# Softmax sums reciprocated through a DRAM scratch and multiplied on GpSimd, a first head put in place by engines, and a new plan

## Chip, cores and metric

The kernel runs on one NeuronCore of one Trainium2 chip. The metric is the device time of one launch in microseconds (us), 781.72 before as the median of three runs (781.61 to 781.91). Lower is better. The engines are called PE (TensorE), DVE (VectorE), ACT (ScalarE), POOL (GpSimd) and SP (SyncE, which here only issues DMAs).

## The reference

Two batches of eight attention heads, 768 positions, 64 columns, with a mask by hash bucket, and then two feed-forward blocks on the 1536 x 512 result:

```python
q_bits = (np.einsum('bhsd,dk->bhsk', q, proj) > 0)          # 6 bits, the same for k
mask = q_bucket[:, :, :, None] == k_bucket[:, :, None, :]
scores = np.where(mask, scale * np.matmul(q, k.transpose(0, 1, 3, 2)), -1e9)
attn = np.exp(scores - np.max(scores, axis=-1, keepdims=True))
attn = attn / (np.sum(attn, axis=-1, keepdims=True) + 1e-09)
x = (attn @ v).transpose(0, 2, 1, 3).reshape(1536, 512)
...
h = x @ w_in;  x = (h * np.tanh(softplus(h))) @ w_out         # block 1, 512 -> 2048 -> 512
h = x @ w_in2; y = elu(h) @ w_out2                            # block 2
```

## The kernel before, in words

**Precision.** Every fp32 operand is split into a high part rounded to fp32r and the rest, and a product is two or three matmuls over these parts. So each tensor needs a cast (line 231 on ACT, 233 on DVE and POOL) and a subtraction (`sub`, line 236).

**A head.** There are 16 heads in 8 pairs. `prepare(g)` loads k and q of head g, transposed, into `rw`, splits them into `z` (two parts), and forms `qkt`, four slots of 128 x 768 in which k and q parts are stacked for the score matmuls. Rows of `z` must change partitions for that, so four DMAs copy them (line 350, `qkt<-z`); for head 0 the four are shared between the queues of SP and ACT. The projection `pj` (line 363, six matmuls) gives the hash bits, which DVE turns into mask rows: for head 0 straight into `qkt` by four instructions (`direct`, line 370), for the others into `bits` (line 376), from which four DMAs (line 382) carry them to `qkt`.

**A tile.** `tile_ops(i)` handles 128 queries, six tiles to a head: four score matmuls into PSUM (`st`, line 418), the maximum on DVE (`pt`, line 421), its negative (`nb`, line 424), and the exponential on ACT (line 426), which also writes the row sum into a column of `sm`. After a head's last tile DVE adds 1e-9 to the six sums (line 434) and takes reciprocals (`rc`, line 437), and POOL spreads `rc` over 64 columns (`rb`, line 440). `value_ops` works on two tiles: transposes (`tu`, line 468), split by ACT and DVE into `pth` and `ptl`, and value matmuls (`xt`, line 481), which ACT copies into `xr` (line 501).

**A pair of heads.** The value result of a head lies in two halves over the partitions. DMAs carry halves to `xs` and `xr` (lines 507, 511, 513), POOL adds them (line 515). Then PE transposes `rb` into PSUM (`r`, line 493, three transposes for each half of 768 columns), DVE multiplies `r` onto `xr` (line 522), and `xr` is split into `x_hi` and `x_lo`, the operands of the first feed-forward block. The last two heads (`late`) do this in pieces of two tiles.

**Feed-forward.** Weights come in 64 units, fetched as int64 pairs and rebuilt by ACT, DVE and POOL. `h` (line 593) is 2304 matmuls of 128 x 512.

**Order.** Nothing is scheduled by hand. `Plan.run` simulates five in-order engines with the costs given to `p.op`, picks by priority (tile number plus the offsets in `OFF` and `ODD`), and writes each engine's instructions in that order. On the chip each engine runs its list strictly in order and waits on semaphores, so an instruction that waits holds up all behind it.

Of the kernel before, what the change touches and what calls it, by code (L numbers as in the profile page):

```python
# [35 lines left out]
WARM = 10  # L36
HOLD = 16
NEARLY = 3
# [3 lines left out]
WAIT = {'PE': 150, 'ACT': 0, 'DVE': 50, 'POOL': 50, 'SP': 100}  # L42
OFF = {'rh': 27.75, 'cp': -6.25, 'ld': 29.75, 'sp': 10.0, 'pj': -5.5, 'bits': -10.0, 'mk': 41.25, 'v': -55.25, 'S': -2.5, 'max': 1.25, 'exp': 15.0, 'sum': 1.25, 'T': 0.0, 'hi': -8.25, 'lo': 1.75, 'R': -10.0, 'pv': 4.0, 'xc': -12.75, 'xa': -5.75, 'xn': -33.75, 'xh': 30.25, 'xm': 29.0}
ODD = {'lo': [-2.0, -0.5, -2.5, -7.5, -7.0, 1.5], 'T': [-4.5, 1.5, 0.5, 2.0, 11.0, 0.5], 'pv': [5.5, 1.5, 2.5, -0.5, -6.0, 0.0], 'exp': [0.0, 1.5, -3.0, 1.5, 4.0, -4.5], 'hi': [3.0, 1.0, -2.5, 0.5, 6.5, 0.0], 'S': [-0.5, 1.5, 1.0, 0.0, -1.0, 0.0], 'xc': [4.0, 1.0, 7.0, 0.0, 2.5, -1.5], 'max': [1.0, 9.0, -1.0, -0.5, 1.0, 0.0]}
PE, ACT, DVE, POOL, SP = "PE", "ACT", "DVE", "POOL", "SP"
# [131 lines left out]

CH = {'rh': ('POOL',), 'v': ('POOL',), 'xh': ('ACT', 'POOL'), 'eps': ('DVE',)}

# [7 lines left out]
def kernel(ctx, tc, qk, v, w, tab, out):  # L187
    nc = tc.nc
# [97 lines left out]

    def attention(p, ap, pss, pst, psx, h_r):
        ident = ap.tile([128, 128], F32, name="ident")
# [45 lines left out]
        def prepare(g):  # L334
# [14 lines left out]
            def move(out, in_):  # L349
                return lambda e: (nc.scalar if e == ACT else nc.sync).dma_start(out=f32(out()), in_=f32(in_()))  # L350
            two = {SP: 650, ACT: 400} if g == 0 else {SP: 650}
            deps = [p.op(two, move(lambda: wt.tile[0:64, 0:2], lambda: z.tile[64:128, 0:1].to_broadcast([64, 2, S])),
                         [h], [z, wt], at('cp'), lat=4600),
                    p.op(two, move(lambda: wt.tile[64:128, 2], lambda: z.tile[0:64, 0]), [h], [z, wt], at('cp'), lat=4600),
                    p.op(two, move(lambda: wt.tile[0:64, 2:4], lambda: z.tile[0:64, 0:2]), [lo], [z, wt], at('cp'), lat=4600),
                    p.op(two, move(lambda: wt.tile[64:128, 0], lambda: z.tile[64:128, 1]), [lo], [z, wt], at('cp'), lat=4600)]
            pj = Buf(xt_r, f"pj{g}")
# [9 lines left out]
            if g == 0:  # L367
# [4 lines left out]
                for c, k in ((0, 1), (1, 1), (0, 0), (1, 0)):  # L372
                    deps.append(p.op({DVE: dve(HS)}, lambda e, c=c, k=k: direct(e, c, k), [o], [pj, wt], at('bits')))
            else:
# [13 lines left out]
            if g % 2 == 0:  # L388
# [9 lines left out]
                V[g // 2] = (vr, vt, ld, lo)  # L398

        def tile_ops(i):  # L400

# [4 lines left out]
            if t == 0:  # L406
                SM[g] = Buf(sm_r, f"sm{g}"), []
                RC[g] = Buf(rc_r, f"rc{g}")
            if g % 2 == 0 and t == 0:
                RB[g // 2] = Buf(rb_r, f"rb{g}"), {}  # L410
            sm, sums = SM[g]
            rc = RC[g]
            rb, ready = RB[g // 2]
# [16 lines left out]
            rest.append((pt, o))  # L430
            late = g >= BH - 2
            if t == NQ - 1 or late and t % 2:
                r = slice(t - 1 if late else 0, t + 1)
                s = p.op(pick('eps', {DVE: 70, POOL: 250}), lambda e: eng(e).tensor_scalar(
                    out=sm.tile[:, r], in0=sm.tile[:, r], scalar1=1e-9, scalar2=None, op0=ALU.add),
                    sums[r], [sm], order(i, 'sum'))
                s = p.op({DVE: 76}, lambda e: nc.vector.reciprocal(out=rc.tile[:, r], in_=sm.tile[:, r]),
                         [s], [sm, rc], order(i, 'sum'))
                n = r.stop - r.start
                s = p.op({POOL: 150 + 50 * n}, lambda e: nc.gpsimd.tensor_copy(  # L440
                    out=rb.tile[:, r, g % 2], in_=rc.tile[:, r].unsqueeze(2).to_broadcast([128, n, 64])),
                    [s], [rc, rb], order(i, 'sum'))
                for j in range(r.start, r.stop):
                    ready.setdefault(j, []).append(s)
            if t % 2 == 1:
# [6 lines left out]
        def value_ops(i):  # L452
# [31 lines left out]
            pv_op = x  # L484
            rb, ready = RB[g // 2]

            def spread(name, ts, after):

                r = Buf(xt_r, name)

                def run(e):
                    for j, tt in enumerate(ts):
                        nc.tensor.transpose(r.tile[:, j * 128:(j + 1) * 128],
                                            rb.tile[:, tt].rearrange("p h d -> p (h d)"), ident)
                return r, p.op({PE: 108 * len(ts)}, run, [after] + [d for tt in ts for d in ready[tt]], [rb, r], order(i, 'R'))
            b, kt = divmod(g // 2, NX)
            if g < BH - 2:
                if t == 1:
                    XR[g] = (Buf(xr_r, f"xr{g}"), [])
                xr, parts = XR[g]  # L500
                parts.append(p.op({ACT: act(TH)}, lambda e: copy(e, xr.tile[:, cs], xt.tile[:, 0:TH]), [x], [xt, xr],
                                  order(i, 'xc')))
                if t < NQ - 1:
                    return
                if g % 2 == 0:
                    xs = Buf(xs_r, f"xs{g}")
                    XS[g // 2] = xs, p.op({SP: 650}, lambda e: nc.sync.dma_start(out=xs.tile[0:64], in_=xr.tile[64:128]),
                                          parts, [xr, xs], order(i, 'xm'), lat=3000)
                    return
                xe, (xs, m) = XR[g - 1][0], XS[g // 2]  # L510
                m2 = p.op({SP: 650}, lambda e: nc.sync.dma_start(out=xs.tile[64:128], in_=xr.tile[64:128]),
                          parts, [xr, xs], order(i, 'xm'), lat=3000)
                m = p.op({SP: 650}, lambda e: nc.sync.dma_start(out=xe.tile[64:128], in_=xr.tile[0:64]),
                         parts + [m], [xr, xe], order(i, 'xm'), lat=3000)
# [3 lines left out]
                norms = []  # L518
                for c in range(2):
                    r, o = spread(f"r{i}_{c}", range(3 * c, 3 * c + 3), a)  # L520
                    hc = slice(c * HS, (c + 1) * HS)
                    norms.append(p.op({DVE: dve(HS)}, lambda e, r=r, hc=hc: nc.vector.tensor_tensor(  # L522
                        out=xe.tile[:, hc], in0=r.tile[:, 0:HS], in1=xe.tile[:, hc], op=ALU.mult), [a, o], [xe, r], order(i, 'xn')))
                h = p.op(pick('xh', {ACT: act(S, False), DVE: 500, POOL: 830}), lambda e: copy(e, x_hi[:, kt, to], xe.tile),
                         norms, [xe], order(i, 'xh'))
# [39 lines left out]

        first = []
        last, gates = [], []
        setup()
        prepare(0)
        for i in range(len(steps)):  # L570
# [136 lines left out]
    with tc.manual_schedule():  # L707
        p = Plan()
        with ExitStack() as low:
            with ExitStack() as att, ExitStack() as scores:  # L710
                def space_pool(stack, name, bufs, space=None, **kw):
                    return stack.enter_context(tc.tile_pool(name=name, bufs=bufs, **({"space": space} if space else {}), **kw))
                ap = space_pool(att, "ap", 1)
                pst = space_pool(att, "pst", TB, PSUM)
                psx = space_pool(att, "psx", 4 - TB, PSUM)
# [12 lines left out]
                h_r = Ring(6, bank)  # L728
                attention(p, ap, pss, pst, psx, h_r)
                ta = p.run()  # L730
# [54 lines left out]
```

## Time and profile before

| | |
|---|---|
| median of three runs | 781.72 us |
| the profiled execution, whole | 781.22 us |
| its span, first to last instruction | 779.4 us |
| PE busy | 761.2 us (98%) |
| DVE, ACT, POOL busy | 602.6, 416.6, 287.0 us |
| mean granted TensorE clock | 0.993 of 2.4 GHz |
| attention, to where `h` runs unbroken | 0 to 259.49 us |
| feed-forward, unbroken matmuls | 516.20 us |

The span is what the trace covers; 1.8 us of the whole time lie outside it. A profile lists when each instruction started and how long it took. "Idle before" is the time in which its engine had nothing running, with the instruction whose semaphore ended it. PE instructions are pipelined: a matmul's duration is longer than the step from its start to the next one's.

### The profile page before, as it was taken

Reading aid. Unit: us, or ns where it says so; the run is one execution under the profiler, and the core shown is the slowest. Engines: PE = TensorE matmul, PEld = TensorE weight load, DVE = VectorE, ACT = ScalarE, POOL = GpSimd, SP = SyncE. Lnnn points to the kernel's source line nnn. Section 1 sums busy time; section 2 is a strip of 40 time slices with the busy share of each in tenths; the row PEclk is TensorE's granted clock in tenths of the full one; section 3 lists DMA queues with packets and bytes.
Section 4 is the critical chain, followed back from the end, with each engine's and each line's share of the span. In section 5 each row is a group of like instructions: output and inputs, shape, how many; then the busy total and the mean of one; then the engine's idle time right before and its main releaser. Section 6 shows DMA issues by size and latency. Waiting matters only on the chain.

```text
span 779.4 us, 11177 instructions
## 1 busy us (share of the span) xinstructions
PE 761.2 (98%) x4010; PEld 660.3 (85%) x4010; DVE 602.6 (77%) x1107; ACT 416.6 (53%) x800; POOL 287.0 (37%) x228
## 2 busy tenths in 40 slices
PE   7999999999899999999999999999999999999998
PEld 6999898998897888888888888888888888888886
DVE  4899898988799865456677766899976789989852
ACT  1797787777687654453333434357555444444420
POOL 1625427516214242322323223873233332333320
PEclk9999999999999999999999999999999999999999
DMA  8664663763451221212111221012221112121112
GB/s 208 175 183 124 177 165 108 193 152 78 106 140 37 75 89 55 81 56 82 54 55 55 81 82 55 27 59 77 81 82 56 54 57 80 59 77 55 54 68 94
DMA packets 23863, 70.98 MB, mean 91 GB/s; under 512 B 3824, under 2 KB 4544, under 8 KB 23808
## 3 DMA queue, kind: packets, MB, share of 16 engines
q1 hardware_dynamic: 23504, 69.67, 30.1%
q10 hardware_dynamic: 304, 0.60, 0.4%
q8 instruction: 31, 0.51, 0.3%
q14 instruction: 24, 0.20, 0.1%
HBM read 43.00 MB, written 3.15 MB: 59 GB/s over the span
## 4 chain that ended last, share of the span: by engine, by line
PE 85%; DVE 6%; DMA 4%; ACT 3%; POOL 2%; issue 1%; SPq 0%; POOLq 0%; ACTq 0%; DVEq 0%
PE h L593 67%; PE st L418 6%; PE xt L481 6%; PE tu L468 5%; DVE pt L421 2%; DVE ptl L236 2%; ACT pt L426 1%; PE pj L363 1%; POOL xr L515 1%; DMA xr<-xr 1%; DMA qkt<-z 1%; ACT pth L473 1%; DMA xs<-xr 1%; DVE xr L522 1%; DMA cst<-in_tab_dram 0%
## 5 line engine op out<-in xcount | busy, mean ns | idle before, releaser
L236 POOL TENSOR_TENSOR wt<-wt,whi 128x512 f32<-128x512 f32 x64 | 84.0, 1313 | 319.6 <-ACT whi L231 305.5
L593 PE MATMUL h<-x_hi,whi 128*128 128x512 f32 x384 | 149.6, 390 | 0.0
L593 PE MATMUL h<-x_hi,wlo 128*128 128x512 f32 x384 | 149.4, 389 | 0.0
L593 PE MATMUL h<-x_lo,whi 128*128 128x512 f32 x384 | 149.4, 389 | 0.0
L593 PE MATMUL h<-glo,whi 128*128 128x512 f32 x384 | 149.4, 389 | 0.0
L593 PE MATMUL h<-ghi,wlo 128*128 128x512 f32 x384 | 149.4, 389 | 0.0
L593 PE MATMUL h<-ghi,whi 128*128 128x512 f32 x384 | 149.4, 389 | 0.0
L426 ACT ACTIVATE pt<-pt,nb 128x768 f32<-128x768 f32 x96 | 90.5, 945 | 28.0 <-DVE nb L424 27.9
L265 ACT ACTIVATE ws<-wraw 128x512 f32<-128x512 f32 x64 | 43.4, 679 | 114.9 <-POOL wlo L283 112.8
L236 DVE TENSOR_TENSOR ptl<-tu,pth 128x512 fp32r<-128x512 f32 x144 | 94.8, 684 | 8.4 <-ACT pth L473 7.6
L421 DVE TENSOR_SCALAR_CACHE_REDUCE pt<-st 128x768 f32<-128x768 f32 x96 | 89.9, 950 | 11.0 <-PE st L418 10.1
L418 PE MATMUL st<-qkt 76*128 76x384 f32 (+1 forms) x384 | 86.3, 355 | 9.7 <-DVE pt L421 6.2
L473 ACT CAST pth<-tu 128x512 fp32r<-128x512 f32 x144 | 80.2, 586 | 18.2 <-PE tu L468 17.9
L283 POOL TENSOR_TENSOR wlo<-wt,ws 128x512 fp32r<-128x512 f32 x64 | 86.5, 1352 | 5.5 <-DVE ws L278 0.9
L236 DVE TENSOR_TENSOR glo<-h,ghi 128x512 fp32r<-128x512 f32 x96 | 65.2, 686 | 28.6 <-ACT ghi L231 28.4
L693 DVE TENSOR_TENSOR y_acc<-h,y_acc 128x512 f32<-128x512 f32 x72 | 48.3, 687 | 48.2 <-PE h L593 48.2
L593 PEld LDWEIGHTS h<-glo,whi 128*128 128x128 f32 x384 | 72.1, 188 | 15.3 <-DVE glo L236 0.2
L593 PEld LDWEIGHTS h<-ghi,whi 128*128 128x128 f32 x384 | 72.1, 188 | 15.0
L593 PEld LDWEIGHTS h<-x_hi,wlo 128*128 128x128 f32 x384 | 72.1, 188 | 15.0 <-POOL wlo L283 0.2
L593 PEld LDWEIGHTS h<-x_lo,whi 128*128 128x128 f32 x384 | 72.1, 188 | 14.7
L593 PEld LDWEIGHTS h<-ghi,wlo 128*128 128x128 f32 x384 | 72.1, 188 | 14.7
L593 PEld LDWEIGHTS h<-x_hi,whi 128*128 128x128 f32 x384 | 72.1, 188 | 14.6
(68 smaller groups left out, 1260.2 us busy)
## 6 DMA issues: line engine op xcount, KB each, us to landing
wraw<-in_w_dram SPq DMA_DIRECT2D x64, 512.0 KB
qkt<-z SPq DMA_DIRECT2D x31, 384.0 KB
rw<-in_qk_dram SPq DMA_DIRECT2D x16, 384.0 KB
qkt<-z SPq DMA_DIRECT2D x31, 192.0 KB
vr<-in_v_dram SPq DMA_DIRECT2D x8, 384.0 KB
out_dram<-y_acc SPq DMA_DIRECT2D x12, 256.0 KB
xs<-xr SPq DMA_DIRECT2D x14, 192.0 KB
xr<-xr SPq DMA_DIRECT2D x7, 192.0 KB
```

What stands on the lines that cost most here:

```text
L236: eng(e).tensor_tensor(out=out, in0=a, in1=b, op=ALU.subtract)
L265: o1 = p.op({ACT: act(n, False)}, lambda e: nc.scalar.activation(out=s.tile, in_=high().bitcast(F32), func=AF.Square), [ld], [raw, s], prio)
L283: o9 = p.op({POOL: pool(n)}, lambda e: nc.gpsimd.tensor_tensor(out=flat(lo), in0=t.tile, in1=s.tile, op=ALU.add), [o6, o8], [t, s, lo], prio)
L363: nc.tensor.matmul(pj.tile[:, 0:HS], lhsT=sp[:, b, 64 * (1 - c):64 * (1 - c) + 128], rhs=z.tile[:, a, c * HS:(c + 1) * HS], start=(n == 0) ...
L418: nc.tensor.matmul(st.tile[:, c, 0:HS], lhsT=wt.tile[0:n, q, t * 128:(t + 1) * 128], rhs=wt.tile[0:n, 2 + q, c * HS:(c + 1) * HS], start=( ...
L421: o = max_op = p.op({DVE: dve(S)}, lambda e: nc.vector.tensor_scalar(out=half(pt.tile), in0=st.tile[:, :, 0:HS], scalar1=-MASKED / SCALE, ...
L426: o = p.op({ACT: act(S, False) + 196}, lambda e: nc.scalar.activation(out=pt.tile, in_=pt.tile, func=AF.Exp, bias=nb.tile, scale=SCALE, ac ...
L468: nc.tensor.transpose(tu.tile[:, k, j], pt.tile[:, (2 * b + k) * 128:(2 * b + k + 1) * 128], ident)
L473: o = p.op({ACT: act(512)}, lambda e, tu=tu, ks=ks: nc.scalar.copy(out=hi.tile[:, ks], in_=flat(tu)), [o], [tu, hi], order(i, 'hi'))
L481: nc.tensor.matmul(xt.tile[:, 0:TH], lhsT=vt.tile[:, k, g % 2], rhs=m.tile[:, k], start=(k == 0 and j == 0), stop=(k == NKT - 1 and j == 1))
L593: nc.tensor.matmul(t.tile, lhsT=a.tile[:, k], rhs=r, start=(k == 0 and j == 0), stop=(k == 3 and j == 2))
L693: y = p.op({DVE: dve(n)}, lambda e, ya=ya, t=t: nc.vector.tensor_tensor(out=ya, in0=t.tile, in1=ya, op=ALU.add), [x, Y[m, c]], [t], prio)
```

## The change

**Normalisation.** For heads 0 to 13 the reciprocals no longer pass through POOL's copy, PE's transposes and DVE's multiplication. SP writes `rc` (128 partitions x 6) to a row of a DRAM scratch `dr`, in pieces of 24 bytes, and reads the row back, broadcast to 64 partitions, into `rr`. POOL multiplies `rr` onto `xr` (768 columns, read with a step of six elements). The cast to `x_hi` is POOL's alone. The last two heads keep the old way.

**Row sums.** The 1e-9 is added by two instructions on half the columns each.

**First head.** ACT casts k and half of q straight into `qkt`, DVE casts the low parts, and only the second half of the q columns comes by two smaller DMAs, which tiles 3 to 5 wait for (`later`). The fourth mask instruction is likewise waited for by tiles 3 to 5 alone. The filling matmuls `hold` fall from 16 to 8 and follow `pj` of head 0 instead of head 1.

**Plan.** `OFF` and `ODD` have new numbers, and some planned DMA costs are longer.

```diff
-HOLD = 16
+HOLD = 8
-OFF = {'rh': 27.75, 'cp': -6.25, ...
+OFF = {'rr': 40.0, 'rh': 45.25, 'cp': 32.75, ...
-CH = {'rh': ('POOL',), 'v': ('POOL',), 'xh': ('ACT', 'POOL'), 'eps': ('DVE',)}
+CH = {'rh': ('POOL',), 'v': ('POOL',), 'xh': ('POOL',)}
...
+            for r, slot, src, n, c in ((k, 2, k, S, w), (q, 2, k, S, w), (k, 0, q, q1, half_w), (k, 1, q, q1, half_w)):
+                deps.append(p.op({ACT: c}, cast(r, slot, lambda src=src: rw.tile[src], n), [ld], [rw, wt], -60))
+            deps.append(p.op({DVE: 500}, cast(k, 3, lambda: f32(z.tile[k, 1]), S), [lo], [z, wt], -45))
+            deps.append(p.op({DVE: 280}, cast(q, 0, lambda: f32(z.tile[q, 1]), q1), [lo], [z, wt], -45))
+            later.append(p.op({SP: 650}, lambda e: nc.sync.dma_start(
+                out=f32(wt.tile[0:64, 0:2, tail]), in_=f32(z.tile[64:128, 0:1, tail].to_broadcast([64, 2, S - q1]))),
+                [h], [z, wt], -45, lat=4600))
+            later.append(p.op({SP: 650}, lambda e: nc.sync.dma_start(
+                out=f32(wt.tile[64:128, 0, tail]), in_=f32(z.tile[64:128, 1, tail])), [lo], [z, wt], -45, lat=4600))
...
-            o = first_op = p.op({PE: 700}, scores, wdeps, [wt, st], order(i, 'S'))
+            o = first_op = p.op({PE: 700}, scores, wdeps + (later if g == 0 and t >= NQ // 2 else []), [wt, st], order(i, 'S'))
...
+                    s = p.op({SP: 700}, lambda e: nc.sync.dma_start(
+                        out=dr.tile[j:j + 1].rearrange("o (p t) -> p (o t)", p=128), in_=rc.tile), [s], [rc, dr],
+                        order(i, 'rr'), lat=4000)
+                    ready.append(p.op({SP: 650}, lambda e: nc.sync.dma_start(
+                        out=rr.tile[64 * j:64 * j + 64], in_=dr.tile[j:j + 1].to_broadcast([64, S])), [s], [dr, rr],
+                        order(i, 'rr'), lat=4000))
...
-                for c in range(2):
-                    r, o = spread(f"r{i}_{c}", range(3 * c, 3 * c + 3), a)
-                    norms.append(p.op({DVE: dve(HS)}, lambda e, r=r, hc=hc: nc.vector.tensor_tensor(
-                        out=xe.tile[:, hc], in0=r.tile[:, 0:HS], in1=xe.tile[:, hc], op=ALU.mult), [a, o], [xe, r], order(i, 'xn')))
+                a = p.op({POOL: pool(S)}, lambda e: nc.gpsimd.tensor_tensor(
+                    out=turned(xe), in0=turned(xe), in1=rr.tile.rearrange("r (p t) -> r t p", p=128), op=ALU.mult), [a] + ready, [xe, rr], order(i, 'xn'))
...
-                p.op({PE: 175 * HOLD}, lambda e: spin(HOLD, hold), [kv[1][2]], [hold], -40)
+                p.op({PE: 175 * HOLD}, lambda e: spin(HOLD, hold), [kv[0][2]], [hold], -40)
```

On PE, at the start of the program, these rows stood before (`st0` to `st5` are the six tiles of head 0, `pj1` is head 1's projection):

```order
L563 MATMUL warm_89<-x_lo_65 128x384 x10
L363 MATMUL pj0_120<-z0_109,sp_82 128x384 x6
L363 MATMUL pj1_131<-z1_111,sp_82 128x384 x6
L563 MATMUL hold_143<-x_lo_65 128x384 x16
L418 MATMUL st0_169<-qkt0_114 128x384 x4
L418 MATMUL st1_176<-qkt0_114 128x384 x4
L418 MATMUL st2_190<-qkt0_114 128x384 x4
```

and these stand there now:

```order
L601 MATMUL warm_91<-x_lo_65 128x384 x10
L367 MATMUL pj0_119<-z0_113,sp_84 128x384 x6
L601 MATMUL hold_134<-x_lo_65 128x384 x8
L445 MATMUL st0_153<-qkt0_111 128x384 x4
L445 MATMUL st1_159<-qkt0_111 128x384 x4
L367 MATMUL pj1_167<-z1_130,sp_84 128x384 x6
L445 MATMUL st3_178<-qkt0_111 128x384 x4
L445 MATMUL st4_191<-qkt0_111 128x384 x4
```

Head 1's projection has moved behind two tiles of head 0, and tile 3 comes before tile 2. On DVE, where the first pair of heads is normalised, these rows stood before (`xr0` is the pair's `xr`, `r11` the transposed reciprocals):

```order
L236 TENSOR_TENSOR ptl17_816<-tu17_1_820,pth17_802 128x512
L522 TENSOR_TENSOR xr0_377<-r11_0_843,xr0_377 128x384
L522 TENSOR_TENSOR xr0_377<-r11_1_855,xr0_377 128x384
L236 TENSOR_TENSOR ptl17_816<-tu17_2_831,pth17_802 128x512
L236 TENSOR_TENSOR ptl19_883<-tu19_0_861,pth19_872 128x512
```

and these now, with nothing of `xr` among them:

```order
L236 TENSOR_TENSOR ptl17_807<-tu17_1_811,pth17_793 128x512
L236 TENSOR_TENSOR ptl17_807<-tu17_2_819,pth17_793 128x512
L448 TENSOR_SCALAR pt21_817,mx21_816<-st21_802 128x768
L448 TENSOR_SCALAR pt22_852,mx22_851<-st22_835 128x768
L448 TENSOR_SCALAR pt23_868,mx23_867<-st23_846 128x768
```

The two multiplications are gone from between the `ptl`. In SP's queue, around the same heads, these rows stood before (`xs` and `xr` the pair's halves, `bits` the mask rows of a later head):

```order
L507 DMA xs_925<-xr_774 64x768
L382 DMA qkt_885<-bits_997 12x384 x4
L342 DMA rw_1055<-in_qk_dram 128x768
L350 DMA qkt_1101<-z_756 64x2x768
L350 DMA qkt_1101<-z_756 64x768
```

and these now:

```order
L548 DMA xs_941<-xr_766 64x768
L477 DMA dr_769<-rc_970 128x6
L387 DMA qkt_888<-bits_997 12x384 x4
L480 DMA rr_844<-dr_769 64x768
L344 DMA rw_1062<-in_qk_dram 128x768
L352 DMA qkt_1103<-z_791 64x2x768
L352 DMA qkt_1103<-z_791 64x768
```

The write to the scratch is ahead of the four mask DMAs, its reading back is behind them, and the next head's load and operands follow.

## Rows read from the trace of the kernel before

**Rows 1.** The page: busy us, share of the span, instructions.

```profile
PE 761.2 (98%) x4010; PEld 660.3 (85%) x4010; DVE 602.6 (77%) x1107; ACT 416.6 (53%) x800; POOL 287.0 (37%) x228
```

**Rows 2.** The chain that ended last: start us, us, what.

```profile
0.74 3.33 DMA cst<-in_tab_dram
6.71 7.95 DMA qkt<-z
16.79 5.63 PE st L418 x16
25.03 1.07 PE pj L363 x6
26.10 0.88 PE tu L468 x8
111.09 6.46 DMA xs<-xr
259.49 516.20 PE h L593 x2277
```

**Rows 3.** Windows: busy us (x instructions) of PE, PEld, DVE, ACT, POOL; PEclk.

```profile
16.00:23.00 7.00, 6.81 (x23) 5.80 (x22) 5.43 (x15) 3.89 (x8) 3.11 (x3) 0.51 0.70 205
40.00:80.00 40.00, 40.00 (x307) 39.30 (x306) 37.41 (x93) 34.06 (x74) 15.59 (x13) 1.00 0.57 152
80.00:215.00 135.00, 127.76 (x939) 123.44 (x938) 117.39 (x283) 102.43 (x219) 59.51 (x47) 0.99 0.55 139
```

**Rows 4.** Timeline, 0 to 25 us: start, duration, engine, operation [idle before].

```profile
4.61 0.55 DVE L233 CAST z<-rw 128x768 fp32r<-128x768 f32 x1
5.20 0.96 DVE L236 TENSOR_TENSOR z<-rw,z 128x768 fp32r<-128x768 f32 x1
5.00 0.83 ACT L231 CAST z<-rw 128x768 fp32r<-128x768 f32 x1 [2.54 <-DMA rw<-in_qk_dram]
6.87 2.77 DVE L370 TENSOR_SCALAR qkt<-pj,cst 12x384 fp32r<-12x384 f32 x4 [0.71 <-PE pj L363]
16.65 0.95 DVE L421 TENSOR_SCALAR_CACHE_REDUCE pt<-st 128x768 f32<-128x768 f32 x1
14.79 1.81 PE L418 MATMUL st<-qkt 128*128 128x384 f32 x8 [3.50 <-DMA qkt<-z]
14.44 2.43 SPq L382 DMA_DIRECT2D qkt<-bits  x3
23.36 1.67 PE L418 MATMUL st<-qkt 128*128 128x384 f32 x8
```

**Rows 5.** Waits, 0 to 260 us: who waited for whom, us, times, longest.

```profile
DVE xr L522 <- POOL xr L515: 9.5, 5, 3.5
POOL xr L515 <- DMA xr<-xr: 19.6, 3, 13.9
```

**Rows 6.** Timelines of POOL, DVE and PE where one pair is normalised.

```profile
175.14 1.84 POOL L515 TENSOR_TENSOR xr<-xr,xs 128x768 f32<-128x768 f32 x1 [13.89 <-DMA xr<-xr]
...
177.01 0.56 DVE L522 TENSOR_TENSOR xr<-r,xr 128x384 f32<-128x384 f32 x1 [1.99 <-POOL xr L515]
...
178.59 0.95 PE L418 MATMUL st<-qkt 128*128 128x384 f32 x4 [1.34 <-DVE pt L421]
```

**Rows 7.** Groups, 0 to 260 us: shapes, count | busy us, mean ns | idle before.

```profile
L493 PE MATMUL r<-ident,rb 128*128 128x128 f32 x48 | 7.8, 273 | 0.4 <-DVE xr L522 0.4
L522 DVE TENSOR_TENSOR xr<-r,xr 128x384 f32<-128x384 f32 x14 | 7.6, 552 | 9.5 <-POOL xr L515 9.5
L434 DVE TENSOR_SCALAR sm<-sm 128x6 f32<-128x6 f32 x14 | 2.3, 162 | 0.2
```

**Rows 8.** Timelines of DVE, SP and PE around one head's reciprocals.

```profile
100.77 0.18 DVE L437 RECIPROCAL rc<-sm 128x6 f32<-128x6 f32 x1
...
100.88 3.13 SPq L382 DMA_DIRECT2D qkt<-bits  x4
105.44 0.33 SPq L342 DMA_DIRECT2D rw<-in_qk_dram  x1
107.77 3.21 SPq L350 DMA_DIRECT2D qkt<-z  x4
...
125.70 1.57 PE L418 MATMUL st<-qkt 128*128 128x384 f32 x8
```

More of the change, by code (lines that the diff above doesn't have):

```diff
@@ L285, in convert, with attention @@
         WT[u] = (hi, lo, o9)
-    def attention(p, ap, pss, pst, psx, h_r):
+    def attention(p, ap, dp, pss, pst, psx, h_r):
         ident = ap.tile([128, 128], F32, name="ident")
@@ L349, in move @@
             def move(out, in_):
[L350 to L356, printed above, removed]
+                return lambda e: nc.sync.dma_start(out=f32(out()), in_=f32(in_()))
+            if g == 0:
+                deps = place(wt, rw, z, ld, h, lo)
+            else:
+                deps = [p.op({SP: 650}, move(lambda: wt.tile[0:64, 0:2], lambda: z.tile[64:128, 0:1].to_broadcast([64, 2, S])),
+                             [h], [z, wt], at('cp'), lat=4600),
+                        p.op({SP: 650}, move(lambda: wt.tile[64:128, 2], lambda: z.tile[0:64, 0]), [h], [z, wt], at('cp'), lat=4600),
+                        p.op({SP: 1250}, move(lambda: wt.tile[0:64, 2:4], lambda: z.tile[0:64, 0:2]), [lo], [z, wt], at('cp'), lat=4600),
+                        p.op({SP: 650}, move(lambda: wt.tile[64:128, 0], lambda: z.tile[64:128, 1]), [lo], [z, wt], at('cp'), lat=4600)]
             pj = Buf(xt_r, f"pj{g}")
@@ L372, in prepare @@
                 for c, k in ((0, 1), (1, 1), (0, 0), (1, 0)):
-                    deps.append(p.op({DVE: dve(HS)}, lambda e, c=c, k=k: direct(e, c, k), [o], [pj, wt], at('bits')))
+                    (deps if c == 0 or k == 1 else later).append(p.op(
+                        {DVE: dve(HS)}, lambda e, c=c, k=k: direct(e, c, k), [o], [pj, wt], at('bits')))
             else:
@@ L398, in prepare, with place, cast @@
                 V[g // 2] = (vr, vt, ld, lo)
+        def place(wt, rw, z, ld, h, lo):
+            q1 = HS
+            k, q = slice(0, 64), slice(64, 128)
+            def cast(r, slot, src, n):
+                return lambda e: copy(e, wt.tile[r, slot, 0:n], src()[:, 0:n])
+            w = act(S, False)
+            half_w = act(q1, False)
+            deps = []
+            for r, slot, src, n, c in ((k, 2, k, S, w), (q, 2, k, S, w), (k, 0, q, q1, half_w), (k, 1, q, q1, half_w)):
+                deps.append(p.op({ACT: c}, cast(r, slot, lambda src=src: rw.tile[src], n), [ld], [rw, wt], -60))
+            deps.append(p.op({DVE: 500}, cast(k, 3, lambda: f32(z.tile[k, 1]), S), [lo], [z, wt], -45))
+            deps.append(p.op({DVE: 280}, cast(q, 0, lambda: f32(z.tile[q, 1]), q1), [lo], [z, wt], -45))
+            tail = slice(q1, S)
+            later.append(p.op({SP: 650}, lambda e: nc.sync.dma_start(
[3 more added lines that the diff above has]
+                out=f32(wt.tile[64:128, 0, tail]), in_=f32(z.tile[64:128, 1, tail])), [lo], [z, wt], -45, lat=4600))
+            return deps
         def tile_ops(i):
@@ L408, in tile_ops @@
                 RC[g] = Buf(rc_r, f"rc{g}")
+            late = g >= BH - 2
             if g % 2 == 0 and t == 0:
-                RB[g // 2] = Buf(rb_r, f"rb{g}"), {}
+                RB[g // 2] = (Buf(rb_r, f"rb{g}"), {}) if late else (Buf(dr_r, f"dr{g}"), Buf(rr_r, f"rr{g}"), [])
             sm, sums = SM[g]
             rc = RC[g]
-            rb, ready = RB[g // 2]
             def scores(e):
@@ L430, in tile_ops @@
             rest.append((pt, o))
-            late = g >= BH - 2
             if t == NQ - 1 or late and t % 2:
                 r = slice(t - 1 if late else 0, t + 1)
-                s = p.op(pick('eps', {DVE: 70, POOL: 250}), lambda e: eng(e).tensor_scalar(
-                    out=sm.tile[:, r], in0=sm.tile[:, r], scalar1=1e-9, scalar2=None, op0=ALU.add),
-                    sums[r], [sm], order(i, 'sum'))
+                n = (r.stop - r.start) // 2
+                eps = [p.op({DVE: 70}, lambda e, x=x: nc.vector.tensor_scalar(
+                    out=sm.tile[:, x], in0=sm.tile[:, x], scalar1=1e-9, scalar2=None, op0=ALU.add),
+                    sums[x], [sm], order(i, 'sum')) for x in (slice(r.start, r.start + n), slice(r.start + n, r.stop))]
@@ L437, in tile_ops @@
                 s = p.op({DVE: 76}, lambda e: nc.vector.reciprocal(out=rc.tile[:, r], in_=sm.tile[:, r]),
[L438 to L444, printed above, removed]
+                         eps, [sm, rc], order(i, 'sum'))
@@ new lines, in tile_ops @@
+                if late:
+                    rb, ready = RB[g // 2]
+                    n = r.stop - r.start
+                    s = p.op({POOL: 150 + 50 * n}, lambda e: nc.gpsimd.tensor_copy(
+                        out=rb.tile[:, r, g % 2], in_=rc.tile[:, r].unsqueeze(2).to_broadcast([128, n, 64])),
+                        [s], [rc, rb], order(i, 'sum'))
+                    for j in range(r.start, r.stop):
+                        ready.setdefault(j, []).append(s)
+                else:
+                    dr, rr, ready = RB[g // 2]
+                    j = g % 2
+                    s = p.op({SP: 700}, lambda e: nc.sync.dma_start(
[4 more added lines that the diff above has]
+                        order(i, 'rr'), lat=4000))
@@ L484, in value_ops, with turned @@
             pv_op = x
-            rb, ready = RB[g // 2]
+            def turned(x):
+                return x.tile.rearrange("r (t p) -> r t p", p=128)
             def spread(name, ts, after):
+                rb, ready = RB[g // 2]
                 r = Buf(xt_r, name)
@@ L517, in value_ops @@
                 to = slice(b * S, (b + 1) * S)
[L518 to L523 removed]
+                rr, ready = RB[g // 2][1:]
+                a = p.op({POOL: pool(S)}, lambda e: nc.gpsimd.tensor_tensor(
+                    out=turned(xe), in0=turned(xe), in1=rr.tile.rearrange("r (p t) -> r t p", p=128), op=ALU.mult), [a] + ready, [xe, rr], order(i, 'xn'))
                 h = p.op(pick('xh', {ACT: act(S, False), DVE: 500, POOL: 830}), lambda e: copy(e, x_hi[:, kt, to], xe.tile),
[L525 removed]
+                         [a], [xe], order(i, 'xh'))
                 XD[b, kt] = [p.op({POOL: pool(S)}, lambda e: sub(
@@ L564, in spin @@
                                  start=True, stop=True)
-        first = []
+        first, later = [], []
         last, gates = [], []
@@ L713 @@
                 ap = space_pool(att, "ap", 1)
+                dp = space_pool(att, "dp", 1, bass.MemoryType.DRAM)
                 pst = space_pool(att, "pst", TB, PSUM)
@@ L728 @@
                 h_r = Ring(6, bank)
-                attention(p, ap, pss, pst, psx, h_r)
+                attention(p, ap, dp, pss, pst, psx, h_r)
                 ta = p.run()
```

18 lines of the change are left out of this document (10 added, 8 removed).

## The prediction

> **What bounds the kernel.** I read the page first: PE is busy for 761.2 us, 98% [rows 1], but a pipelined engine can be busy and still lose steps, so that figure does not settle it. The chain of waits does: its last piece is 516.20 us of unbroken feed-forward matmuls from 259.49 on [rows 2]. Nothing in the change touches them, so the time can only move by where that piece begins. I then looked at attention in windows. From 40 to 80 us PE is busy for 40.00 of 40 us and starts 307 matmuls, one in 0.130 us; there PE alone sets the pace, although DVE is close behind with 37.41 us [rows 3]. From 80 to 215 us the pace breaks: 939 matmuls, where 135 us at the earlier pace hold 1036. The 97 missing ones are worth 12.6 us. The reader is to see two kinds of time there: PE's work, which shrinks only when instructions go, and steps lost to others. A third kind stands at the start: the first score matmul waits until 14.79 us for a DMA [rows 4].
>
> **What the lost steps hang on.** DVE waited five times, 9.5 us in all, for POOL's addition of the two halves, and POOL had waited for the DMAs that bring them [rows 5]. One case in full: POOL sits idle for 13.89 us until the DMA lands, adds until 176.98, DVE stands for 1.99 us in front of its multiplication, and PE then idles 1.34 us for the next maximum [rows 6]. DVE is held in order, so the maxima and `ptl` behind the multiplication are late too, and with 37.41 of 40 us used it cannot catch up.
>
> **Term 1, the start.** k and q of head 0 are in SBUF at 4.61 us. Before, four DMAs carried the parts over, and the last landed at 14.66 (6.71 + 7.95) [rows 2]. Now DVE does a cast and a subtraction as before, to 6.16 [rows 4]; then a cast of 768 columns (at most 0.55, the same number of columns on 128 rows) and one of 384 (0.28, half of it), to 6.99; then three of the four mask instructions at 2.77/4 = 0.69 [rows 4], to 9.07. ACT's four casts take 0.83 + 0.83 + 0.42 + 0.42 from 4.61, to 7.11, and are covered. With 0.2 for the semaphore the first score matmul starts at 9.3, 5.5 us earlier. Against it, the projection of head 1, six matmuls of 1.07 us [rows 2], is still to be done behind tile 1. For it, the sixteen score matmuls that took 5.63 us at a granted clock of 0.51 [rows 2, 3] would take 16 x 1.07/6 = 2.85 at full clock; DVE's maxima of 0.95 each [rows 4] then set the pace, so I take 2.0 of these 2.8 us. That makes 6.4 us.
>
> I count it a second way, at head 1's first score, which was at 23.36 [rows 4]. Its mask DMAs now wait for bits that DVE makes behind two maxima, at 9.3 + 1.0 + 1.9 + 0.7 = 12.9; four issues of 2.43/3 us [rows 4] end at 16.1, and a small DMA took 3.3 us from issue to landing [rows 2], so the last is there at about 18.6 (issued at 15.3). DVE's six maxima, the bits and the six negatives end at about 17.7 (10.3 + 6 x 0.95 + 0.7 + 6 x 0.16, the last by the small addition [rows 7]). Head 1 begins some 4.7 us earlier, with head 2's projection and four transposes (1.5 us) already done, which stood behind it before: 6.2 us. I take **6.0 us**, with 4 and 7.5 as ends: the two tail DMAs that tile 3 now needs before tile 2, issued by about 6.9, must land by about 11.7, and a landing as slow as the 6.46 us of the slowest piece in the chain [rows 2] would cost 1.6.
>
> **Term 2, PE's work.** 42 of the 48 transposes of reciprocals go; six belong to the last heads [rows 7]. Eight such transposes step in 0.88 us [rows 2], so 42 x 0.11 = **4.6 us**, all of it on the engine that sets the pace. The dropped filling matmuls stood in idle time and count nothing.
>
> **Term 3, the lost steps.** DVE loses its 14 multiplications, 7.6 us, and with them the 9.5 us of waiting [rows 7]. It gains 14 additions of 0.16 us, 2.3 us at most [rows 7]. POOL takes seven multiplications over. Their strided read has no row; a contiguous one takes 1.84 us [rows 6], so 12.9 us, and twice that if the step halves its rate. POOL is busy for 59.51 of 135 us [rows 3], and nothing in attention reads `x_hi` or `x_lo`; either value is covered. What is late next would be what stands behind POOL: casts of later heads' `z`, which have a head and more of lead, and SP's queue, below. So the 12.6 us can return whole or not at all. As 40 to 80 us holds a pair's normalisation as well and lost nothing, whole is possible; but every offset of the plan is new, and a new order brings its own late DMAs. I leave a third of the loss standing, 4.2 us, and take **8.4 us**, with 4 and 12.6 as ends.
>
> **Sum.** The profiled execution took 781.2, and 781.2 - 6.0 - 4.6 - 8.4 = 762.2. The median of the runs lies 0.5 above that execution, which makes 762.7; I forecast **763.0 us**. The ends of the three terms give 769 (4 + 4.6 + 4 = 12.6 us saved) and 757 (7.5 + 4.6 + 12.6 = 24.7 saved).
>
> **Rival: the waits move.** The plan's new order may lose as much as the old one, on another engine; DVE, at 94% of 40 to 80 us [rows 3], is the candidate. Then term 3 is nothing and the time is 781.7 - 10.6 = 771. Against it speaks that all five waits have one cause [rows 5]; for it, that they followed a plan too.
>
> **Rival: the start stays at half clock.** PE was idle for 3.50 us before 14.79, and from 16 to 23 us the granted clock was 0.51, the lower of the two levels [rows 3, 4]. Now PE idles about 1 us before the first score and then a little behind each maximum. If this too lowers the clock, term 1 loses its 2.0 us: 765. The Trainium skill (TensorE: Matmul & The Clock Gate, section "A second HAM failure mode: psum-queue depth-cycling") says that frequent short idles between matmul groups make the clock swing between its levels; by that rule this rival is right. From 40 to 80 us short steps between engines left the clock at 1.00 [rows 3], so by the trace it stays high, and I keep the 2.0.
>
> **Rival, slower: SP stands still.** The reading back of `dr` waits for its write, and the next head's load and operand DMAs stand behind it. In one head, the reciprocals were ready at 100.95, mask issues took 3.13, the load 0.33, and the operands went out from 107.77 to 110.98; the tiles that need them began at 125.70 [rows 8]. With 0.8 us for each new issue, as for a mask's [rows 4], the write may take 107.77 - 100.95 - 0.33 - 0.8 - 0.8 = 4.9 us without moving anything, and another 125.70 - 110.98 - 6.46 = 8.3 us before PE waits. A transfer in 128 small pieces, the table's, took 3.33, the slowest piece 6.46 [rows 2]. To come out above 781.7, 14 heads must each lose 19/14 = 1.4 us, so each write must take some 15 us. The Trainium skill (DMA: Bandwidth & Descriptors, section Specifications) says that transfers under 512 bytes are done by read-modify-write. No run here shows such a write, and that sentence changes none of these numbers.
>
> **Rival: no change.** Were feed-forward held by its weights, an earlier end of attention would be spent waiting, and the time stays at 781.7. Its matmuls run without a gap from 259.49 [rows 2], so nothing holds them now; with 19 us less of attention that is not proven.
>
> **Chances.** Forecast 0.60, waits move 0.17, half clock 0.14, slower 0.05, no change 0.04. A measurement of this kernel tells about 0.2%, 1.6 us, from no change, so faster is 0.91, same 0.04, slower 0.05. The range leaves out the slower and the unchanged case and little else: 757.5 to 772.
>
> **What will show it.** Term 1: the first score matmul near 9.3 us, head 1's near 18.6, a granted clock of 1.00 up to 25 us. Term 2: six `r` transposes on PE. Term 3: no DVE wait on POOL's addition, some 7.5 matmuls in a us from 80 to 215 us. Together: feed-forward unbroken from about 241 us, and 516 us long. I am wrong if PE waits for operand or mask DMAs in mid-attention, if DVE waits for POOL in a new place, or if that last piece grows.

## The result, and the profile after

The changed kernel takes **771.59 us** as the median of four executions (769.01 to 771.67), against 781.82 for the kernel before on the same chip: a ratio of 0.9861, with a 95% interval of 0.9840 to 0.9882. On another chip, later, five executions gave 767.09 (766.44 to 769.46) and a ratio of 0.9813 (0.9796 to 0.9829). So it is 10 to 15 us faster, where 18.7 were forecast. The profiled execution took 769.0 us, 12.2 less than that of before; it is the fastest of the four, and the median lies 2.6 us above it.

The page of the changed kernel, part 1 (busy us, share of the span, instructions), answers to [rows 1]:

```profile
PE 750.9 (98%) x3960; PEld 650.5 (85%) x3960; DVE 606.8 (79%) x1115; ACT 417.6 (54%) x799; POOL 298.3 (39%) x226
```

DVE has lost 7.6 us of multiplications and is nonetheless busy for 4.2 us more. From the chain that ended last (start, us, what), as in [rows 2]:

```profile
74.91 8.60 DMA wraw<-in_w_dram
...
247.41 516.23 PE h L631 x2277
```

The feed-forward piece has kept its length and begins 12.1 us earlier, not 18.7. Timeline of PE at the start of the changed kernel, as in [rows 4]:

```profile
8.23 0.51 PE L445 MATMUL st<-qkt 128*128 128x384 f32 x2
9.43 1.30 PE L445 MATMUL st<-qkt 76*128 76x384 f32 x6 [0.69 <-DVE qkt L374]
...
18.18 0.94 PE L445 MATMUL st<-qkt 128*128 128x384 f32 x4
```

The first scores start at 8.2 and go on at 9.4, when the mask is there; head 1's start at 18.18. The start does what was forecast. Windows of the changed kernel (busy us x instructions of PE, PEld, DVE, ACT, POOL; granted clock; DMA), as in [rows 3]:

```profile
16.00:23.00 7.00, 6.67 (x51) 6.14 (x50) 6.06 (x18) 5.82 (x14) 3.90 (x3) 1.00 0.83 204
40.00:80.00 40.00, 39.19 (x294) 38.19 (x293) 36.68 (x89) 32.58 (x71) 17.25 (x12) 1.00 0.71 179
80.00:215.00 135.00, 128.17 (x950) 123.74 (x949) 126.01 (x297) 105.00 (x224) 71.21 (x49) 1.00 0.63 153
```

From 16 to 23 us the clock is at its upper level and PE starts 51 matmuls where it started 23. In mid-attention there is no such gain: 950 matmuls from 80 to 215 us against 939, and 40 to 80 us, unbroken before, now has gaps. DVE has become dense there: it is busy for 126.0 of 135 us, up from 117.4. Waits from 0 to 260 us (who for whom, us, times, longest), against [rows 5], and groups on DVE, POOL and PE (count | busy us, mean ns | idle before), against [rows 7]:

```profile
PE tu L506 <- DVE ptl L236: 8.2, 9, 1.9
DVE ptl L236 <- ACT pth L511: 8.4, 14, 2.8
```

```profile
L461 DVE TENSOR_SCALAR sm<-sm 128x3 f32<-128x3 f32 x28 | 14.6, 538 | 0.0
L461 DVE TENSOR_SCALAR sm<-sm 128x1 f32<-128x1 f32 x12 | 1.3, 141 | 0.2 <-ACT pt L453 0.2
L451 DVE TENSOR_SCALAR nb<-mx 128x1 f32<-128x1 f32 x96 | 12.8, 146 | 0.4
L560 POOL TENSOR_TENSOR xr<-xr,rr 128x768 f32<-128x768 f32 x7 | 15.8, 2261 | 0.5
L534 PE MATMUL r<-ident,rb 128*128 128x128 f32 x6 | 1.2, 281 | 0.0
```

DVE's wait for POOL's addition is gone. In its place PE waits nine times for DVE's `ptl`. The row to look at is the first group: an addition of three columns takes 0.54 us on average, and one of a single column 0.14. Twenty-eight additions cost 14.6 us where 28 x 0.16 = 4.5 were to be expected. The timeline around one pair of them shows what runs beside them:

```profile
91.38 1.85 POOL L236 TENSOR_TENSOR x_lo<-xr,x_hi 128x768 fp32r<-128x768 f32 x1
...
92.30 0.15 DVE L451 TENSOR_SCALAR nb<-mx 128x1 f32<-128x1 f32 x1
92.36 0.90 DVE L461 TENSOR_SCALAR sm<-sm 128x3 f32<-128x3 f32 x1
...
93.17 1.85 POOL L236 TENSOR_TENSOR vt<-vr,vt 128x768 fp32r<-128x768 f32 x1
93.17 0.14 DVE L451 TENSOR_SCALAR nb<-mx 128x1 f32<-128x1 f32 x1
...
93.24 1.81 DVE L461 TENSOR_SCALAR sm<-sm 128x3 f32<-128x3 f32 x1
...
95.19 1.25 DVE L236 TENSOR_TENSOR ptl<-tu,pth 128x512 fp32r<-128x512 f32 x2
...
95.89 1.25 PE L506 MATMUL tu<-ident,pt 128*128 128x128 f32 x8 [1.35 <-DVE ptl L236]
```

Each addition ends when the POOL instruction that was running ends (93.26 and 93.23; 95.05 and 95.02). `nb`, one column, takes 0.14 us beside the same POOL instruction. `ptl` stands behind the additions, and PE behind `ptl`. All eight additions above 0.5 us end within 0.03 us of the end of a subtraction on POOL. Theory A is therefore: the addition waits for POOL's running instruction, and that is where the forecast gain went. Theory B: DVE is late because the new order gives it its work in bursts, and the additions only show it.

### The profile page after: what moved, and what is told of

It reads as the page before. It is cut to its first block, busy times and chain, and to the rows that moved or that the text cites. A ratio compares the mean times of both kernels' runs of the same rounds, so it can differ in the third digit from the quotient of the medians.

```text
span 767.2 us, 11108 instructions
## 1 busy us (share of the span) xinstructions
PE 750.9 (98%) x3960; PEld 650.5 (85%) x3960; DVE 606.8 (79%) x1115; ACT 417.6 (54%) x799; POOL 298.3 (39%) x226
## 4 chain that ended last, share of the span: by engine, by line
PE 81%; DVE 13%; ACT 2%; DMA 2%; issue 1%; SPq 0%; ACTq 0%; DVEq 0%
PE h L631 68%; DVE pt L448 5%; DVE ptl L236 5%; PE st L445 4%; PE tu L506 4%; PE xt L519 4%; ACT pt L453 1%; DMA wraw<-in_w_dram 1%; DVE sm L461 1%; ACT pth L511 1%; PE pj L367 1%; DMA cst<-in_tab_dram 0%; DVE nb L451 0%; SPq L352 0%; DVE wt L270 0%
## 5 line engine op out<-in xcount | busy, mean ns | idle before, releaser
L453 ACT ACTIVATE pt<-pt,nb 128x768 f32<-128x768 f32 x96 | 90.5, 945 | 12.1 <-DVE nb L451 11.9
L506 PE MATMUL tu<-ident,pt 128*128 128x128 f32 x576 | 80.7, 275 | 8.8 <-DVE ptl L236 8.2
```

Of the source, the lines that this page charges most:

```text
L453: o = p.op({ACT: act(S, False) + 196}, lambda e: nc.scalar.activation(out=pt.tile, in_=pt.tile, func=AF.Exp, bias=nb.tile, scale=SCALE, ac ...
L506: nc.tensor.transpose(tu.tile[:, k, j], pt.tile[:, (2 * b + k) * 128:(2 * b + k + 1) * 128], ident)
```

## The experiments

Each ratio is to the kernel before on the same chip, with its 95% interval.

### The additions: left out, in single columns, stepped, as one

A row sum holds exp(0) = 1, so 1e-9 is lost in fp32; e1 leaves the addition out, the other three compute everything.

```diff
-                eps = [p.op({DVE: 70}, lambda e, x=x: nc.vector.tensor_scalar(
-                    out=sm.tile[:, x], in0=sm.tile[:, x], scalar1=1e-9, scalar2=None, op0=ALU.add),
 e1:
+                eps = [p.op({DVE: 70}, lambda e, x=x: None,
 e2, e3, e4, each with its pieces y:
+                eps = [p.op({DVE: 70}, lambda e, x=x: [nc.vector.tensor_scalar(
+                    out=sm.tile[:, y], in0=sm.tile[:, y], scalar1=1e-9, scalar2=None, op0=ALU.add) for y in ...
+e2                  (slice(c, c + 1) for c in range(x.start, x.stop))],
+e3                  ((x,) if late else (slice(0, NQ, 2), slice(1, NQ, 2)) if x.start else ())],
+e4                  ((x,) if late else (r,) if x.start else ())],
```

> The addition of 1e-9 to the row sums is left out (both instructions of every head); every other instruction of the changed kernel stands where it stood on every engine. Theory A (the 128x3 addition on DVE waits until POOL's running instruction is over): the 14.6 us of the 28 additions go, and with them PE's lost steps behind them at 64, 96, 99, 152, 181 and 209 us (0.98, 1.52, 0.74, 0.77, 2.06, 0.43 us: 6.5 together); the loss at 85 us behind ACT's wait for the weights stays. Some of it will be lost elsewhere: 4 to 6 us faster than the changed kernel, 763 to 765 beside its profiled 769.0, and a median of about 766 beside 771.6. Rival B (DVE is late because the new order gives it its work in bursts; the additions are only where it shows): DVE is relieved of 28 x 0.16 = 4.5 us of work, most of it where PE does not wait, and the kernel gains under 1.5 us.

> The same sums, but each addition of three columns (two in the last heads) is three (two) of one column: 84 and 12 instructions of 0.14 us, as the 12 of one column took in the changed kernel, where none took longer. Theory A: no addition above 0.2 us; DVE's 14.6 us for 28 become 11.8 for 84, so its work hardly falls, but no instruction stands for 1.8 us any more; 2 to 5 us faster than the changed kernel, about 767 as a median. Rival B: DVE has 84 x 0.14 instead of 28 x 0.16 us of real work, 7 us more; no gain, or some us slower.

> Two additions of three columns per head as in the changed kernel, but of columns 0, 2, 4 and of 1, 3, 5 (a step of 8 bytes), both where the second stood. Theory A in the form that it is the dense three columns which make DVE wait for POOL: 0.16 us each, none long, and nearly the time of the kernel without additions, 1 us above it at most. Theory A in the form that any instruction over more than one column waits: one of each two is still up to 1.8 us, and the time is between 767 and 771. Rival B: as the changed kernel, 771.

> One addition of all six columns per head, as the kernel before had it, where the second of the two stood. Theory A: it meets POOL's instructions as the two did, up to 1.8 us, but once per head instead of twice: about half of the 10.1 us that the 28 lose, so 2 to 3 us faster than the changed kernel, about 769 as a median. If the split in two was harmless the time stays within 1 us of 771.6, and the additions last 0.16 us each. Rival B: within 1 us of the changed kernel, no matter how long they last.

| | median us | ratio (95%) |
|---|---|---|
| e1, left out | 761.57 | 0.9722 (0.9701 to 0.9744) |
| e2, single columns | 763.38 | 0.9743 (0.9723 to 0.9762) |
| e3, stepped | 767.13 | 0.9788 (0.9762 to 0.9814) |
| e4, one of six | 765.53 | 0.9771 (0.9750 to 0.9792) |

Without the additions, the window from 80 to 215 us and the chain's last piece are these:

```profile
80.00:215.00 135.00, 133.27 (x991) 130.71 (x989) 121.78 (x292) 110.25 (x236) 70.26 (x48) 0.99 0.64 159
```

```profile
240.54 516.25 PE h L631 x2277
```

POOL is nearly as busy as in the changed kernel (70.3 us against 71.2), and PE starts 41 matmuls more. The additions one column at a time, from the view of their line (duration in ns least/median/greatest, first and last start):

```profile
L461 DVE TENSOR_SCALAR sm<-sm x96: 127/143/155, 18.8 to 238.8; 128x1 f32<-128x1 f32 x96
```

Ninety-six instructions, none above 0.155 us, and the kernel is 5.5 us faster than the changed one by the ratios 0.9743 and 0.9813 (9.2 against 0.9861). Under theory B more instructions on DVE had to cost time. The same view with a step of two columns, and with all six at once:

```profile
L461 DVE TENSOR_SCALAR sm<-sm x40: 127/158/1832, 22.0 to 242.8; 128x3 f32<-128x3 f32 x28, 128x1 f32<-128x1 f32 x12
```

```profile
L461 DVE TENSOR_SCALAR sm<-sm x26: 127/157/1756, 22.7 to 241.6; 128x6 f32<-128x6 f32 x14, 128x1 f32<-128x1 f32 x12
```

A step does not help: the long ones stay. Six at once are as long as three but half as many (8.1 us in all for 14). So the wait belongs to an addition of more than one column, whatever its step, and the split in two that the change made cost more waits: eight of its 28 took over 0.5 us, 10.1 us in all beyond 28 x 0.16, where here six of 14 took over 0.3 us, 5.9 us beyond 14 x 0.16. Theory A holds and B falls; my size was too small, since e1 gained 7.1 us over the changed kernel by the ratios 0.9813 and 0.9722, not 4 to 6.

The Trainium skill (SBUF — State Buffer, section "Who interferes with whom") says that DVE and GpSimd share a pair of ports as an exclusive lock that is held for a whole instruction, and that DVE takes it in a two-port mode, which `tensor_scalar` can enter, or with two SBUF inputs. The durations agree: the additions of three and of six columns waited to the end of POOL's instruction, and `ptl`, with one input in PSUM, took 0.68 us beside POOL and without it. Why one column did not wait, no run here shows.

### The changed kernel again

No edit.

> The changed kernel itself, unaltered, in more executions. In the kernels without the additions, in columns, stepped and of six, PE stood still for 1.7 to 1.9 us near 84 us behind ACT's wait for the first weights, and the granted clock then was 0.50 for some 3.3 us. The changed kernel's profile has the same standstill at 84 us and no such stretch, but its three other executions showed a mean clock of 0.996 to 0.998 and took 2.6 us longer. If that stretch is what they had, executions fall into two groups: about 769 at a clock of 1.000 and about 771.6 at 0.996, and a profile at 0.996 shows the stretch behind 85 us. Otherwise the half clock stands elsewhere, or the time spreads evenly.

767.09 us, ratio 0.9813 (0.9796 to 0.9829). The additions took 12.3 us here. The forecast of two groups failed: the four executions at a clock of 1.000 range from 766.4 to 769.5, and the one at 0.997 took 768.3. The same order meets POOL's instructions a little differently each time. Its profile, at 0.997, does have the stretch: PE idle for some 1.7 us near 85, then a granted clock of 0.50 from 87 to 89 us. It is not the difference between 771.6 and 767.1, and what that is stays open.

### The parts alone

The kernel before with the first head's part alone; the changed kernel with the old first head.

```diff
 e6: kernel before
+HOLD = 8
+            if g == 0:
+                deps = place(wt, rw, z, ld, h, lo)
...
 e7: changed kernel
+HOLD = 16
-            if g == 0:
-                deps = place(wt, rw, z, ld, h, lo)
```

> The kernel before with the first head's part of the change alone (casts into place, tail DMAs, 8 filling matmuls), before's normalisation and before's offsets. If the predicted 6.0 us of term 1 stand: 775.7 against 781.7, first score near 9.3, head 1's near 18.6, clock 1.00 to 23 us. If what is won at the start is lost again in mid-attention, because DVE or the DMAs set the pace there anyway: 779 to 782, with the start as early.

> The changed kernel with the first head as before (four DMAs, 16 filling matmuls behind head 1's projection); normalisation through the scratch and the new offsets stay. If the parts add up, the changed kernel's loss is that of its start, about 6 us: 775 to 778, first score near 14.8 and a clock of 0.5 from 16 to 23 us. If the first head's gain was swallowed by the later waits for POOL, this kernel is within 2 us of 771.6.

e6: 777.50 us, 0.9941 (0.9921 to 0.9962), that is 4.6 us (3.0 to 6.2) on 781.7, where 6.0 was forecast; its first scores start at 8.16 and head 1's at 18.22, as in the changed kernel. e7: 788.75 us, 1.0084 (1.0066 to 1.0102): slower than before, a plain miss. The planner, given another start, orders every engine otherwise; the edit also gives it the old planned cost, 650 for 1250, of one operand DMA in every later head. PE's waits there:

```profile
PE tu L482 <- DVE nb L427: 5.8, 6, 1.4
PE tu L482 <- DVE ptl L236: 4.8, 3, 3.3
PE st L421 <- DMA qkt<-z: 3.4, 1, 3.4
```

Only the third is the old start; the others are DVE again. The parts do not add up, so the numbers of the plan had to be tried apart from them:

```diff
 e10: changed kernel
+OFF = {'rr': 40.0, 'rh': 27.75, 'cp': -6.25, ...      (before's, and 'rr')
+ODD = {'lo': [-2.0, -0.5, -2.5, -7.5, -7.0, 1.5], ... (before's)
 e12: the same, additions left out as in e1
```

> The changed kernel, both new parts in it, with the offsets that the kernel before had (and 40.0 for the two scratch DMAs, as in the changed kernel). The first head alone with these offsets gave 0.9941 of before, the normalisation alone with the new ones 1.0084. If the new offsets are a fine tuning, this is within 4 us of the changed kernel: 764 to 772. If each engine's order decides which of POOL's instructions meet DVE's, and the new offsets fit only the whole change, then the gain of the two parts is mostly lost: 774 to 786, with the additions long in other places, and PE waiting for DVE or for operand DMAs in mid-attention.

> The kernel with both new parts and the offsets of before, without the additions; all other instructions as in the kernel with the old numbers, where 28 additions took 12.9 us instead of 4.5 and the median was 769.1. Theory A in another order: 4 to 7 us faster than that, 762 to 765. If it was a property of the new offsets that the additions cost PE so much: under 2 us faster, 767 to 769.

e10: 769.13 us, 0.9840 (0.9822 to 0.9858), within the changed kernel's two values. The new numbers give nothing that can be told here. What e7 lost would then be due to these numbers together with the old start and the one planned cost; the old numbers with the old start were not run, so that is not shown. e12: 763.32 us, 0.9750 (0.9731 to 0.9769), so the additions cost 7.0 us in another order too, where 28 took 12.9 us. Windows from 80 to 215 us of e10 and e12:

```profile
80.00:215.00 135.00, 129.83 (x954) 123.18 (x953) 125.61 (x299) 106.39 (x227) 70.60 (x49) 1.00 0.64 157
```

```profile
80.00:215.00 135.00, 133.26 (x988) 128.03 (x987) 121.55 (x287) 109.44 (x235) 70.47 (x50) 1.00 0.65 160
```

With the old `OFF` and `ODD` in both (e10 keeps the change's longer planned DMA costs), the normalisation put on top of the new first head is worth 0.9840 against 0.9941, 7.9 us, with its additions.

### The kernel before without its additions

```diff
-                s = p.op(pick('eps', {DVE: 70, POOL: 250}), lambda e: eng(e).tensor_scalar(
-                    out=sm.tile[:, r], in0=sm.tile[:, r], scalar1=1e-9, scalar2=None, op0=ALU.add),
+                s = p.op(pick('eps', {DVE: 70, POOL: 250}), lambda e: None,
```

The additions of 1e-9 are left out.

> The kernel before with the 14 additions of 1e-9 of its heads 0 to 13 (and those of the last two) left out, all else in its place. Theory A (they cost much only where POOL is busy at that moment; in the kernel before each took 0.16 us): 0 to 2 us faster than before. If any small instruction on DVE at that place costs PE as much as it did in the changed kernel, whatever POOL does, 4 to 6 us faster.

779.80 us, 0.9975 (0.9963 to 0.9988): 2.0 us, the upper end of theory A's span. There all 14 took 0.16 us [rows 7]; no POOL instruction was running at any of them. From the kernel before: a wait of POOL and the additions of the last two heads (both 0 to 260 us), and a piece of the chain that ended last:

```profile
POOL rb L440 <- DVE rc L437: 49.7, 13, 10.2
```

```profile
L434 DVE TENSOR_SCALAR sm<-sm 128x2 f32<-128x2 f32 x6 | 2.3, 386 | 0.0
```

```profile
242.84 1.43 DVE sm L434
```

For ten of the 14, POOL's next instruction was the copy `rb`, which needs the reciprocals that are made behind that very addition: POOL stood idle because it waited for them, and the change took this copy off POOL. The six additions of the last two heads, which e8 leaves out too, are another matter. One of them took 1.51 us, to 244.27, beside a subtraction of POOL that ended at 244.24. So the trace of before already held the price, on the chain that ended last. In e8 feed-forward begins 1.34 us earlier (258.15 against 259.49), about what that one addition had cost. What a small instruction costs depends on who is running beside it.

### ACT's wait for the first weights

```diff
 e9: kernel without additions
-        ... after, [raw], prio=prio, lat=5000)
+        ... after, [raw], prio=prio, lat=9000 if u == 0 else 5000)
```

> The kernel without the additions, and besides ACT's first weight instruction (ws, which waited 3.5 us for the weights' DMA at 80 us) six ACT instructions later in ACT's order; nothing else moves on any engine. In the kernel without the additions alone PE stood still for 1.70 us at 82.2 us behind it and then ran about 3.3 us at a granted clock of 0.50. If the stall is what cost that time, PE's idle time there goes, the granted clock stays at 1.00 through 90 us, and the span falls by 1.9 + 1.7 = 3.6 us, to about 757 from 760.4 (a median of 758 beside 761.6). If DVE was late there for its own work (two conversions with POOL's instructions beside them), PE still waits for ptl near 84 us and the gain is under 1 us. If the clock falls for another reason than the idle time, the stretch at 0.50 stays and the gain is 1.9 at most.

763.38 us, 0.9759 (0.9745 to 0.9773): not faster than e1 (0.9722), rather 2 to 3 us slower. ACT no longer waits for the weights, PE does not stop at 82, and the clock stays at 1.00 to 96 us. But DVE comes to its weight instructions 3.5 us earlier, and they now fall on POOL's. DVE, POOL and PE in e9:

```profile
89.74 1.86 POOL L236 TENSOR_TENSOR x_lo<-xr,x_hi 128x768 fp32r<-128x768 f32 x1
91.54 2.03 POOL L236 TENSOR_TENSOR vt<-vr,vt 128x768 fp32r<-128x768 f32 x1
...
90.21 1.67 DVE L267 TENSOR_SCALAR wt<-wraw 128x512 int32<-128x512 int32 x1
91.91 2.21 DVE L270 SCALAR_TENSOR_TENSOR wt<-wraw,wt 128x512 int32<-128x512 int32 x1
...
95.97 0.66 PE L506 MATMUL tu<-ident,pt 128*128 128x128 f32 x4 [2.72 <-DVE ptl L236]
```

and the same two instructions in e1, where POOL's `vt` had ended at 92.81:

```profile
93.75 0.42 DVE L267 TENSOR_SCALAR wt<-wraw 128x512 int32<-128x512 int32 x1
94.20 0.69 DVE L270 SCALAR_TENSOR_TENSOR wt<-wraw,wt 128x512 int32<-128x512 int32 x1
```

The same wait, by other instructions: 2.8 us more on DVE, 2.72 idle on PE, and a granted clock of 0.50 from 97 to 100 us. The stall that was removed had kept these apart.

### The planner told of the port

```diff
 e11: changed kernel
-                    sums[x], [sm], order(i, 'sum')) for x in ...
+                    sums[x], [sm], order(i, 'sum'), port=True) for x in ...
```

> The changed kernel with all its additions, but the planner is told of them what it is told of the five weight instructions on DVE: that they and POOL's instructions exclude each other. That alters the plan, and with it every engine's order. If the planner's clock is near enough to the chip's, it places the additions between POOL's instructions: the 28 take under 8 us instead of 14.6, and the kernel ends near the one without them, 762 to 766. If its clock is off by more than the gaps between POOL's instructions (the weights landed 8.6 us after their issue began where it counts 5.0), the additions meet POOL as before, 11 to 15 us for 28, and the time is that of the changed kernel, 766 to 771.

774.97 us, 0.9911 (0.9893 to 0.9929). The additions became short, as forecast, but the time lies above both of its ranges. From 0 to 260 us:

```profile
L461 DVE TENSOR_SCALAR sm<-sm 128x3 f32<-128x3 f32 x28 | 5.6, 237 | 0.0
```

```profile
PE tu L506 <- DVE nb L451: 5.4, 5, 1.4
```

The additions take 5.6 us, near the 4.5 of free ones. But the new order has PE wait for DVE in another place, five times, up to 1.4 us, as in e7. Short additions alone do not make a fast kernel; why this order places `tu` so is not settled.

## Why the prediction came out as it did

**What bounds it: right.** The last piece is 516.23 us and begins 12.1 us earlier, all of the profiled gain.

**Term 1: right.** First scores at 8.2 and 9.4 (9.3 forecast), head 1's at 18.18 (18.6), clock 1.00 from 16 to 23 us. Alone it gave 4.6 us (3.0 to 6.2); the forecast 6.0 lies inside that interval.

**Term 2: right in its count.** Six `r` transposes are left; the 4.6 us were not measured alone.

**Term 3: the step that failed.** Its sentence "It gains 14 additions of 0.16 us, 2.3 us at most" took the duration from a kernel in which POOL was idle at that moment, in ten of 14 cases because it waited for the reciprocals itself. The change takes that wait off POOL, and the same paragraph gives POOL more work: it was busy for 71.2 us from 80 to 215 us, up from 59.5. The 28 additions took 14.6 and 12.3 us in the two profiles. As an estimate in matmuls of the profiled execution: without the additions 40 to 80 us holds 303, one in 0.132 us, so 135 us hold 1023. The changed kernel starts 950, a loss of 73 x 0.132 = 9.6 us, and 1.2 more in 40 to 80 us (9 x 0.132). Term 3 thus gave 12.6 - 9.6 - 1.2 = 1.8 instead of 8.4, and 6.0 + 4.6 + 1.8 = 12.4 stands beside the measured 12.2. Without the additions 991 are started, a loss of 4.2 us: the third that I left standing. That kernel's span is 19.0 us shorter than before's (779.4 - 760.4), the sum forecast for the three terms. It leaves out before's additions as well, which are worth 2.0 by e8, so this agreement is good to about 2 us.

**POOL's multiplication: right.** 2.26 us each, between 1.84 and twice that, and no DVE instruction waits for its result. It can hold an addition up like a subtraction, though: in e10 one took 1.99 us and ended 0.04 us after the multiplication beside it.

**Rivals.** *The waits move*: this is nearly what happened. The median stands at its 771, on DVE, the engine that it named; its mechanism, an addition that lasts as long as POOL's instruction, I had not seen. That 771.59 lies inside the range of 757.5 to 772 is luck as far as the sum goes: the sum missed by 8.6 us, and the range reached so far only because it took in this rival. The 767.09 of the other chip lies within the ends of the three terms, 757 to 769. *Half clock at the start*: wrong there. A stretch at 0.50 came later: in e1 PE stood for 1.70 us before 83.94 and the clock was 0.50 from 85 to 88; in the changed kernel's profile it stood for 1.92 us before 85.45 and the clock stayed at 1.00. The rule of the Trainium skill (TensorE: Matmul & The Clock Gate, section "A second HAM failure mode: psum-queue depth-cycling") that stands in that rival did not show at the start; when the clock falls is not settled by these traces. *SP stands still*: wrong. The reading back was issued 3 to 7 us after the write, and PE waited for no operand or mask DMA. *No change*: wrong; feed-forward did not grow.

## What to carry to other kernels

Price a small instruction by what runs beside it in the new order, not by its duration in the old one: here 128x3 took 0.16 us beside an idle POOL and up to 1.99 beside a busy one. When work moves to GpSimd, or a wait is taken off it, look for every DVE instruction that it will now meet, also in the old trace, where one such addition took 1.51 us, and drop those that compute nothing (the 1e-9) or keep them off the port (single columns, or an input in PSUM). The kernel without the additions is the best found, at 0.9722 of before against 0.9813 to 0.9861 for the change; with them in single columns, all computed, it is 0.9743.

## What the runs showed that I had not expected

Three fp32 columns wait for GpSimd and one does not, and a step of 8 bytes makes no difference (1.83 us at most). An instruction's wait for the port is shown as its own duration, not as idle time: the group of additions has 14.6 us busy and 0.0 idle, so no view of waits names POOL. Removing a 3.5 us stall on ACT brought two other instructions onto the port and gave nothing: the kernel was 2 to 3 us slower.
